# VectorE and ScalarE held to program order, softmaxes split in two, in a recurrent-memory attention kernel

## The chip, the cores and the metric

The kernel runs on one core of a Trainium2 chip. The metric is device microseconds of one execution; the figure before is the median of three runs. A separate execution was taken with the profiler, and everything read from a trace comes from that one.

## The reference

Two layers, twice: attention over segments of 32 tokens with 8 memory rows carried from segment to segment, then a gated feed-forward. All are residual, with a layer norm ahead. Sizes: 2048 tokens, width 448, 16 heads of 256, feed-forward width 1792.

```python
for s in range(n_seg):                       # 64 segments, one after another
    h = concat([mem, xs])                    # 8 memory rows + 32 tokens
    q, k, v = h @ Wq, h @ Wk, h @ Wv
    p = softmax(mask(q @ k.T) * scale)
    o = (p @ v) @ Wo
    mem = o[:8]                              # the next segment waits for this
    outs.append(o[8:])

x = x + A(layernorm(x)); x = x + B(layernorm(x))     # B: relu(x Wg) * (x Wu) @ Wd
x = x + A(layernorm(x)); x = x + B(layernorm(x))
```

## The kernel before

**Preparation.** For the first 80 us the kernel folds Wq with Wk and Wv with Wo into A_sb and B_sb (kept in SBUF). Then scores come from `h A h^T` and outputs from `(p h) B`; no separate q, k or v is formed.

**Steps.** The main loop runs 68 steps and a closing one. A step handles one segment of each of two chains: chain 0 is the first attention layer, chain 1 the second, four segments behind. Both share the weights, so one matmul has 80 columns: 2 x (8 + 32) rows. In the first and last four steps only one chain is active. Every second step has a feed-forward block of 128 rows (64 of each chain's), given by a `Feed` object `ff`: such a step is called a feed step here, the other a plain step.

**One step, in TensorE's order.** The heads go in two halves, `hf` 0 and 1.
- `project` (28 tiles a half, in five PSUM banks `BANKS`: tiles 0-5, 6-11, 24-27, 12-17, 18-23) makes `prj`, copied into TQ (tiles 0-23) and TZ (24-27). `project_early` does the narrow fourth chunk of four banks ahead of time in row pairs.
- `hk_make` turns the rows of h (tile kps) and copies them to `hk`.
- `late` is the end of the former step's `weigh_x(1)`, the y products.
- `scores_m` makes Sm, scores of the memory rows' queries; `scores_x` makes Sx, the cross scores of both chains' token rows. Each is followed by a softmax on VectorE and ScalarE: mx, se, exponential, ssum, rs and the weights, PM or PX.
- `flipped` turns the weights (tile pps) and copies them to PT. `weigh_m` multiplies them by hk (tiles ya, yb), `weigh_x` likewise (y1, y2, one for each chain); the results go to Y.
- `project_out` and `project_last` multiply Y by B_sb into ox and o3. From these come the next step's memory rows (in hT) and OT for the residual.

In a feed step the feed-forward comes between: `residual`, `norm` and `xposed` prepare xT; seven units of `gate_up` make ups, gps, the copy ut (ScalarE, two buffers) and hh (VectorE); `down` makes dps, `norm2` normalises for the second chain, `feed_on` puts the rows into hT.

**Order and buffers.** TensorE's order is the program's: `in_order` ties each matmul to the one before. VectorE's and ScalarE's instructions are placed by a scheduler of the language layer, which may take them out of program order; only the two halves of `normed` are pinned. PSUM has eight banks. `bank` gives a tile the bank that by a planned time is free first, where that time is the last matmul's plus `after` ns; a matmul on a bank waits for whoever read its former tile. A softmax was one call:

```python
def weights_of(Sp, n, dst, keep, tag, mask=None):   # mx, se, exp, ssum, rs, weights in one go
```

Of the kernel before, what the change touches and what calls it, by code (L numbers as in the profile page):

```python
# [15 lines left out]
DM = 448  # L16
# [4 lines left out]
SEG = 32  # L21
# [34 lines left out]
def build_kernel(ctx, tc, A_x, A_mem0, A_Wq, A_Wk, A_Wv, A_Wo, B_W_gate, B_W_up, B_W_down, out,  # L56
# [25 lines left out]

    now = [0]
# [38 lines left out]
    def evac(eng, dst, src):  # L122
        if eng is nc.scalar:
            nc.scalar.copy(dst, src)  # L124
        else:
            eng.tensor_copy(dst, src)  # L126
# [17 lines left out]
    nc.vector.tensor_scalar(out=rowi[:, 1:2], in0=rowi[:, 0:1], scalar1=3, scalar2=1,  # L144
                            op0=ALU.arith_shift_right, op1=ALU.bitwise_and)
    nc.vector.tensor_scalar(out=rowi[:, 2:3], in0=rowi[:, 0:1], scalar1=15, scalar2=None,
                            op0=ALU.bitwise_and)
    rowf = glob.tile([P, 3], F32, name="rowf")
    nc.vector.tensor_copy(rowf[:], rowi[:])
# [3 lines left out]
    nc.vector.tensor_copy(keyf[:, 0, :], keyi[:])  # L153
    nc.vector.tensor_scalar(out=keyf[:, 1, :], in0=keyf[:, 0, :], scalar1=-16.0, scalar2=None, op0=ALU.add)
    maskS = glob.tile([P, 4, L], BF, name="maskS")
    nc.vector.memset(maskS[:], 0.0)
    for b in range(4):
        o = 0 if b % 2 == 0 else MEM
        nc.vector.tensor_scalar(out=maskS[:, b, o:o + SEG], in0=keyf[:, b // 2, :], scalar1=rowf[:, 2:3],
                                scalar2=MASKVAL, op0=ALU.is_gt, op1=ALU.mult)  # L160

    blk = glob.tile([P, 2], F32, name="blk")
    nc.vector.tensor_copy(blk[:, 1:2], rowf[:, 1:2])
    nc.vector.tensor_scalar(out=blk[:, 0:1], in0=blk[:, 1:2], scalar1=-1.0, scalar2=1.0,
# [3 lines left out]
    nc.vector.memset(half[:], -0.5)  # L168
# [19 lines left out]
    def row_stats(t):  # L188

        stats = p_ln.tile([P, nc.vector.BN_STATS_DIM], F32, tag="ln_stats")  # L190
        nc.vector.bn_stats(stats[:], t[:])
        mv = p_ln.tile([P, 2], F32, tag="ln_mv")
        nc.vector.bn_aggr(mv[:], stats[:])  # L193
# [5 lines left out]
    def normed(stat):  # L199

        t, mv, rstd = stat
        xn = p_ln.tile([P, 512], BF, tag="ln_xn", bufs=3)
        for a, b, o in ((0, DM, 0), (384, DM, DM)):
            tc.keep_in_program_order(
                nc.vector.tensor_scalar(out=xn[:, o:o + b - a], in0=t[:, a:b], scalar1=mv[:, 0:1],
                                        scalar2=rstd[:], op0=ALU.subtract, op1=ALU.mult))
        return xn
# [21 lines left out]
    def set_mem(g, src, cs):  # L229

        nc.vector.tensor_copy(mem_of(g, cs)[:, 0:src.shape[1]], src)


    with tc.tile_pool(name="pre", bufs=6) as pre:
# [4 lines left out]
        for i in range(6):  # L239
            t = pre.tile([P, 4, 512], BF, name=f"nat{i}", bufs=1)  # L240
            (nc.gpsimd if i % 2 else nc.vector).memset(t[64:128, 3, :], 0.0)
            nats.append(t)
# [16 lines left out]
        spent = {nc.vector: 0.0, nc.scalar: 0.0}  # L259

        def share(dst, src, n, per):
            cost = {nc.vector: 60 + n * per[0], nc.scalar: 170 + n * per[1]}
# [27 lines left out]
        def first_rows():  # L290
# [4 lines left out]
            for b in range(2):  # L295
                rows_in(nc.vector, b, 0, tps0[:, :, block(b)])
# [3 lines left out]
            nc.vector.tensor_copy(mem0T[:], mtp[:])  # L300
# [107 lines left out]
    class Feed:  # L408
# [10 lines left out]
        def residual(self):  # L419
# [3 lines left out]
            nc.vector.tensor_tensor(self.x[:], tp[:].rearrange("p k d -> p (k d)")[:, 0:DM], self.x[:], op=ALU.add)  # L423
# [5 lines left out]
        def xposed(self):  # L429
            tps = transpose_tokens(self.xn)  # L430
            nc.vector.tensor_copy(xT[:], tps[:])

        def gate_up(self, u):
# [10 lines left out]
            nc.scalar.copy(ut[:, :, n], ups[:, :, n])  # L444
            nc.vector.scalar_tensor_tensor(out=hh[:, 2 * u:2 * u + 2, n], in0=gps[:, :, n], scalar=0.0,  # L445
                                           in1=ut[:, :, n], op0=ALU.max, op1=ALU.mult)

        def down(self):
# [4 lines left out]
            if self.first:  # L453
                nc.vector.tensor_tensor(self.nx[TB:P, :], dps[TB:P, 0:DM], self.x[TB:P, :], op=ALU.add)
                self.st = row_stats(self.nx)
                nc.sync.dma_start(xa[(i + 2) % 3][0:TB, :], self.nx[TB:P, :])
                if i + 3 < nblk:
                    nc.sync.dma_start(self.x[TB:P, :], x_dram[block(i + 3)])
            if self.second:
                nc.vector.tensor_tensor(self.x[0:TB, :], dps[0:TB, 0:DM], self.x[0:TB, :], op=ALU.add)  # L460
                nc.sync.dma_start(out_dram[block(i - LAG // BLK)], self.x[0:TB, :])

# [6 lines left out]
        def feed_on(self):  # L469
            if self.first:  # L470
                tps = transpose_tokens(self.xn)
                rows_in(nc.vector, self.i + 2, 1, tps[:, :, TB:P])
                rows_in(nc.scalar, self.i + 2, 0, tps[:, :, 0:TB])
# [22 lines left out]
    def project(hf, chains, hb, j, banks, pre={}):  # L496

        n = L * len(chains)
        for i0, k in banks:
# [8 lines left out]
            if i0 < 24:  # L508
                T = TQ[hf][:].rearrange("p g u w -> p g (u w)")[:, :, 16 * i0:16 * (i0 + k)]
                parts = [(nc.scalar if i0 % 12 else nc.vector, slice(0, P), T)]  # L510
            else:
                parts = [(nc.vector, slice(0, 64), TZ[hf][0:64, :, 0:64]),
                         (nc.scalar, slice(64, 128), TZ[hf][64:128, :, 64:128])]
# [15 lines left out]
    def weights_of(Sp, n, dst, keep, tag, mask=None):  # L529
# [3 lines left out]
        if mask is not None:  # L533
            nc.vector.tensor_tensor(se[:], Sp[:], mask, op=ALU.add)
            Sp = se
        nc.vector.tensor_reduce(mx[:], Sp[:], axis=AX.X, op=ALU.max)  # L536
        nc.vector.tensor_tensor(se[:], Sp[:], mx[:].unsqueeze(2).to_broadcast([P, n, L]), op=ALU.subtract)  # L537
        nc.scalar.activation(se[:], se[:], AF.Exp, scale=SCALE)  # L538
        ssum = main.tile([P, n], F32, tag=f"ssum{tag}", name="ssum")
        nc.vector.tensor_reduce(ssum[:], se[:], axis=AX.X, op=ALU.add)  # L540
        rs = main.tile([P, n], F32, tag=f"rs{tag}", name="rs")
        nc.vector.reciprocal(rs[:], ssum[:])
        if keep is not None:
            nc.vector.tensor_tensor(rs[:], rs[:], keep, op=ALU.mult)
        nc.vector.tensor_tensor(dst[:, :, 0:L], se[:], rs[:].unsqueeze(2).to_broadcast([P, n, L]), op=ALU.mult)

    def flipped(src, n, tag):
# [4 lines left out]
        nc.vector.tensor_copy(PT[:], pps[:].rearrange("p b q -> p (b q)"))  # L552
# [5 lines left out]
    def step(g, ff, pre, late):  # L558
# [12 lines left out]
        def ox_open():  # L571

            nonlocal ox
            ox = bank([P, 3, W], F32, "ox", hold=True) if not end else None

        def hk_make():
            kps = bank([P, 4, 128], BF, "kps")
            for i in range(4):
                tr(kps[:, i, :], hb[:, j, i * HI:(i + 1) * HI], ident[:])
            hk = HK[g % 2]  # L580
            nc.vector.tensor_copy(hk[:].rearrange("p k n -> p (k n)")[:, 0:DM],
                                  kps[:].rearrange("p k n -> p (k n)")[:, 0:DM])
            nc.scalar.copy(hk[:, 4, 64:128], kps[:, 3, 64:128])
            return hk

        def scores_m(hf):
            if not ms:
                return
# [3 lines left out]
            weights_of(Sp, 2, PM[hf], blk[:], f"m{hf}")  # L592

        def scores_x(hf):
            Sp = bank([P, 4, L], F32, "Sx", 900)
# [8 lines left out]
            return Sp  # L604

        def probs_x(hf, Sp):
            weights_of(Sp, 4, PX[hf], None, f"x{hf}", maskS[:] if len(chains) == 2 else None)

        def weigh_m(hf, hk, PT):
# [5 lines left out]
            nc.vector.tensor_copy(YB[hf][:, 0:16, M0:M0 + 16], ya[:].rearrange("p (t q) -> p t q", q=16))  # L615
# [4 lines left out]
            nc.scalar.copy(YB[hf][:, 16:28, M0:M0 + 16], yb[:].rearrange("p (t q) -> p t q", q=16))  # L620

        def weigh_x(hf, hk, PT):
# [14 lines left out]
            for c in chains:  # L637
                keep(nc.scalar if c == 0 else nc.vector, c, 0, y1[c][:])
# [24 lines left out]
        def project_last():  # L663
# [11 lines left out]
            nc.scalar.copy(os[0:64, lo:hi], o3[64:128, lo:hi])  # L675
            if ms:
                m0 = M0 + MEM * ms[0]
                nm = MEM * len(ms)
                nc.scalar.copy(os[64:128, m0:m0 + nm], o3[0:64, m0:m0 + nm])
                for e in range(2):  # L680
                    r = slice(64 * e, 64 * e + 64)
                    nc.vector.tensor_tensor(mem_of(g + 1, ms)[r, 3],
# [8 lines left out]
            for to, x in places:  # L691
                nc.vector.tensor_tensor(OT[r, 3, to:to + SEG], o3[r, x:x + SEG], os[r, x:x + SEG], op=ALU.add)

        def finish():
# [5 lines left out]
            if g == nsteps:  # L700
                nc.scalar.copy(OT[:, 0:3, 0:SEG], ox[:, :, XO[1]:XO[1] + SEG])
# [166 lines left out]
```

## Time and profile before

| what | value |
|---|---|
| median of 3 runs | 1687.98 us (1687.83 to 1688.02) |
| profiled execution | 1692.54 us, span 1690.2 us |
| TensorE matmul busy | 1624.2 us, 96% of the span |
| TensorE weight loads busy | 1484.2 us, 88% |
| VectorE busy | 1146.7 us, 68% |
| ScalarE busy | 661.6 us, 39% |
| granted TensorE clock | 0.993 |

In the groups of instructions, a line names where the operation stands in the code (for most matmuls the helper `mm`, L111, for turns `tr`, L119, for copies `evac`, L124 and L126), its output and inputs, shape and count, then busy time and mean length in ns, then the idle time of its engine just before and what ended it. In the timeline a row has start, length, engine, line and operation, and in brackets the idle time before it. Matmuls are pipelined: each shows as some 200 ns, while the next may start 36 ns later.

### The profile page before, as it was taken

The page shows a single profiled execution, that of the slowest core. Times are in us where ns is not written, and L with a number is a line of the kernel's source. Part 1 is how long each engine was busy: PE and PEld are TensorE (multiplying, and loading weights), DVE is VectorE, ACT ScalarE, POOL GpSimd, SP SyncE. Part 2 cuts the span into 40 slices and gives each one's busy share as a digit, 9 for nine tenths or more (in the row PEclk, how much of TensorE's full clock was granted, in tenths as well). Part 3 has the DMA queues.
Part 4 walks back from the last instruction along what each step waited for, and adds up shares of the span by engine and source line. Part 5 has one row for each costly group of instructions (what it writes and reads, how often), then busy time and mean ns, then how long its engine had stood idle before and what let it go on. Part 6 is the DMA issues. An engine that isn't in the chain of part 4 may idle for free.

```text
span 1690.2 us, 90175 instructions
## 1 busy us (share of the span) xinstructions
PE 1624.2 (96%) x41152; PEld 1484.2 (88%) x41152; DVE 1146.7 (68%) x4037; ACT 661.6 (39%) x1945; POOL 91.0 (5%) x178
## 2 busy tenths in 40 slices
PE   8999999999999999999999999999999999999997
PEld 6688899898988989989889899998889889898886
DVE  6765666776667667766676677666766667666774
ACT  5733433443334334433343334333343344333432
POOL 6200000000000000000000000000000000000000
PEclk9989999999999999999999999999999999999999
DMA  9330000000000000000000000000000000000000
GB/s 257 117 106 19 8 9 9 3 9 9 9 9 9 9 9 5 8 9 9 9 8 9 9 7 5 9 9 9 9 9 9 7 5 9 10 7 6 6 7 6
DMA packets 26782, 33.14 MB, mean 20 GB/s; under 512 B 3352, under 2 KB 24736, under 8 KB 26400
## 3 DMA queue, kind: packets, MB, share of 16 engines
q1 hardware_dynamic: 25312, 23.70, 5.1%
q8 instruction: 321, 5.26, 1.3%
q0 software_dynamic: 1088, 3.68, 0.7%
q14 instruction: 61, 0.50, 0.1%
HBM read 23.70 MB, written 1.84 MB: 15 GB/s over the span
## 4 chain that ended last, share of the span: by engine, by line
PE 80%; DVE 12%; ACT 5%; POOL 1%; issue 1%; ACTq 0%; POOLq 0%; DVEq 0%
PE prj L111 24%; PE ox L111 18%; PE ups L111 6%; PE gps L111 6%; PE dps L111 5%; PE o L111 4%; PE y L111 4%; ACT TQ L124 3%; PE Sx L111 2%; DVE ssum L540 2%; PE pps L119 2%; ACT se L538 2%; PE bps L111 1%; DVE TQ L126 1%; DVE mx L536 1%
## 5 line engine op out<-in xcount | busy, mean ns | idle before, releaser
L111 PE MATMUL prj<-hT,A_sb 128*128 128x80 bf16 (+3 forms) x15232 | 545.4, 199 | 0.1
L111 PEld LDWEIGHTS <-A_sb 128*128 128x128 bf16 (+1 forms) x15232 | 499.5, 99 | 22.8 <-issue 0.8
L111 PEld LDWEIGHTS <-B_sb 128*128 128x128 bf16 (+1 forms) x15232 | 491.1, 103 | 14.1 <-issue 0.4
L111 PE MATMUL ox<-Y,B_sb 128*128 128x80 bf16 (+4 forms) x11424 | 438.9, 199 | 0.3 <-issue 0.3
L126 DVE CAST Y<-y 128x128 bf16<-128x128 f32 (+2 forms) x384 | 156.6, 461 | 60.5 <-PE y L111 57.4
L124 ACT CAST TQ<-prj 128x480 bf16<-128x480 f32 (+2 forms) x304 | 147.6, 496 | 94.9 <-PE prj L111 93.1
L126 DVE CAST TQ<-prj 128x480 bf16<-128x480 f32 (+2 forms) x304 | 170.8, 567 | 14.2 <-PE prj L111 13.9
L124 ACT CAST Y<-y 128x512 bf16<-128x512 f32 (+2 forms) x384 | 144.1, 410 | 63.4 <-DVE Y L126 44.3
L111 PE MATMUL ups<-xT,Wu_sb 128*128 128x128 bf16 (+1 forms) x1904 | 141.0, 218 | 2.4 <-DVE se L537 1.9
L111 PE MATMUL gps<-xT,Wg_sb 128*128 128x128 bf16 (+1 forms) x1904 | 141.2, 218 | 0.0
L111 PEld LDWEIGHTS <-hk 40*128 40x128 bf16 (+1 forms) x1950 | 106.3, 96 | 34.9 <-issue 22.0
L538 ACT ACTIVATE se<-se 128x80 f32<-128x80 f32 (+1 forms) x270 | 80.2, 304 | 87.2 <-DVE se L537 85.3
L111 PEld LDWEIGHTS <-Wu_sb 128*128 128x128 bf16 x1904 | 111.2, 99 | 2.7 <-DVE se L537 2.0
L111 PEld LDWEIGHTS <-Wg_sb 128*128 128x128 bf16 x1904 | 112.9, 99 | 0.0
L675 ACT COPY os<-o 64x80 f32<-64x80 f32 (+3 forms) x68 | 14.8, 218 | 249.9 <-PE o L111 249.9
L444 ACT CAST ut<-ups 128x256 bf16<-128x256 f32 (+1 forms) x238 | 84.4, 355 | 70.1 <-PE ups L111 49.8
L445 DVE SCALAR_TENSOR_TENSOR hh<-gps,ut 128x256 bf16<-128x256 f32 (+1 forms) x238 | 93.1, 401 | 27.5 <-PE gps L111 16.7
L111 PE MATMUL y<-PT,hk 40*128 40x256 bf16 (+1 forms) x1280 | 100.3, 249 | 2.3 <-DVE PT L552 0.3
L195 POOL TENSOR_SCALAR rstd<-mv 128x1 f32<-128x1 f32 x67 | 14.8, 221 | 1533.7 <-DVE mv L193 1484.8
L111 PE MATMUL dps<-Wd_sb,hh 128*128 128x448 bf16 x476 | 95.7, 353 | 0.0
L124 ACT CAST TZ<-prj 64x320 bf16<-64x320 f32 (+2 forms) x152 | 55.9, 378 | 100.0 <-DVE TZ L126 39.0
L540 DVE TENSOR_REDUCE ssum<-se 128x2 f32<-128x80 f32 (+1 forms) x270 | 73.4, 274 | 31.2 <-ACT se L538 26.7
(120 smaller groups left out, 1964.7 us busy)
## 6 DMA issues: line engine op xcount, KB each, us to landing
wo<-in_A_Wo_dram POOLq DMA_DIRECT2D x8, 448.0 KB, 5.6
nat<-in_A_Wq_dram SPq DMA_DIRECT2D x8, 384.0 KB, 5.7
nat<-in_A_Wk_dram SPq DMA_DIRECT2D x8, 384.0 KB, 5.6
nat<-in_A_Wv_dram SPq DMA_DIRECT2D x8, 384.0 KB, 3.9
xa<-in_A_x_dram SPq DMA_DIRECT2D x32, 56.0 KB, 2.6
xa<-xp SPq DMA_DIRECT2D x32, 56.0 KB, 1.9
out_dram<-xa SPq DMA_DIRECT2D x32, 56.0 KB, 2.0
xp<-in_A_x_dram SPq DMA_DIRECT2D x30, 56.0 KB, 2.0
```

Source lines behind the costliest of these rows:

```text
L111: in_order(nc.tensor.matmul(out, lhsT, rhs, **k))
L119: in_order(nc.tensor.transpose(out, src, idn))
L124: nc.scalar.copy(dst, src)
L126: eng.tensor_copy(dst, src)
L195: nc.gpsimd.tensor_scalar(out=rstd[:], in0=mv[:, 1:2], scalar1=EPS, scalar2=None, op0=ALU.add)
L444: nc.scalar.copy(ut[:, :, n], ups[:, :, n])
L445: nc.vector.scalar_tensor_tensor(out=hh[:, 2 * u:2 * u + 2, n], in0=gps[:, :, n], scalar=0.0, in1=ut[:, :, n], op0=ALU.max, op1=ALU.mult)
L536: nc.vector.tensor_reduce(mx[:], Sp[:], axis=AX.X, op=ALU.max)
L538: nc.scalar.activation(se[:], se[:], AF.Exp, scale=SCALE)
L540: nc.vector.tensor_reduce(ssum[:], se[:], axis=AX.X, op=ALU.add)
L675: nc.scalar.copy(os[0:64, lo:hi], o3[64:128, lo:hi])
```

## The change

VectorE and ScalarE calls go through an `InOrder` wrapper that, from the first step of the main loop on, ties each instruction to the one before it on that engine. `weights_of` becomes `softmax`, which returns two functions: the first up to the exponential, the second from the sum to the weights. The step's order is rewritten:

- hk_make moves from behind bank 24 and bank 12 to right behind the first two banks, ahead of `residual`; in feed steps its large copy is ScalarE's.
- `norm` follows the five banks; `norm2` comes right after `down`.
- the memory scores of half 0 stand ahead of half 1's projections instead of behind the first bank; their second part follows two banks of these.
- in feed steps the second parts of the two other softmaxes stand among the first units, PM's turn after unit 3 instead of unit 4, and the second cross softmax after the last unit; in feed steps the copy of the tiles 12-17 of half 1 goes to ScalarE.
- in plain steps the turns and the second parts move as below.
- the two y2 copies of a chain go to one engine; the load of the next x block is written behind the store of the output; planned times of some banks are longer.

```diff
+    class InOrder:
+        def __init__(self, eng):
+            self.eng, self.last, self.on = eng, None, False
...
+            def call(*a, **k):
+                r = f(*a, **k)
+                if self.on:
+                    if self.last is not None:
+                        tc.add_manual_dep(r.ins, self.last,
...
+                    self.last = r.ins.name
+                return r
...
+    dve, act = InOrder(nc.vector), InOrder(nc.scalar)
...
         def down(self):
...
                 nc.sync.dma_start(xa[(i + 2) % 3][0:TB, :], self.nx[TB:P, :])
-                if i + 3 < nblk:
-                    nc.sync.dma_start(self.x[TB:P, :], x_dram[block(i + 3)])
             if self.second:
...
                 nc.sync.dma_start(out_dram[block(i - LAG // BLK)], self.x[0:TB, :])
+            if self.first and i + 3 < nblk:
+                nc.sync.dma_start(self.x[TB:P, :], x_dram[block(i + 3)])
...
-    def project(hf, chains, hb, j, banks, pre={}):
+    def project(hf, chains, hb, j, banks, pre={}, busy=False):
...
-                parts = [(nc.scalar if i0 % 12 else nc.vector, slice(0, P), T)]
+                parts = [(act if i0 % 12 or busy and hf and i0 else dve, slice(0, P), T)]
...
-    def weights_of(Sp, n, dst, keep, tag, mask=None):
+    def softmax(Sp, n, dst, keep, tag, mask=None):
...
+        def first():
+            src = Sp
+            if mask is not None:
+                dve.tensor_tensor(se[:], Sp[:], mask, op=ALU.add)
+                src = se
+            dve.tensor_reduce(mx[:], src[:], axis=AX.X, op=ALU.max)
+            dve.tensor_tensor(se[:], src[:], mx[:].unsqueeze(2).to_broadcast([P, n, L]), op=ALU.subtract)
+            act.activation(se[:], se[:], AF.Exp, scale=SCALE)
+
+        def second():
+            dve.tensor_reduce(ssum[:], se[:], axis=AX.X, op=ALU.add)
+            dve.reciprocal(rs[:], ssum[:])
+            if keep is not None:
+                dve.tensor_tensor(rs[:], rs[:], keep, op=ALU.mult)
+            dve.tensor_tensor(dst[:, :, 0:L], se[:], rs[:].unsqueeze(2).to_broadcast([P, n, L]), op=ALU.mult)
+
+        return first, second
...
-            ox = bank([P, 3, W], F32, "ox", hold=True) if not end else None
+            ox = bank([P, 3, W], F32, "ox", 1400, hold=True) if not end else None
...
-            nc.vector.tensor_copy(hk[:].rearrange("p k n -> p (k n)")[:, 0:DM],
-                                  kps[:].rearrange("p k n -> p (k n)")[:, 0:DM])
-            nc.scalar.copy(hk[:, 4, 64:128], kps[:, 3, 64:128])
+            evac(act if ff is not None else dve, hk[:].rearrange("p k n -> p (k n)")[:, 0:DM],
+                 kps[:].rearrange("p k n -> p (k n)")[:, 0:DM])
+            act.copy(hk[:, 4, 64:128], kps[:, 3, 64:128])
...
-            Sp = bank([P, 2, L], F32, "Sm", 900)
+            Sp = bank([P, 2, L], F32, "Sm", 1100)
...
-            Sp = bank([P, 4, L], F32, "Sx", 900)
+            Sp = bank([P, 4, L], F32, "Sx", 2500 if hf == 0 else 3500 if ff is None else 8000)
...
-                keep(nc.scalar if c == 0 else nc.vector, c, 16, y2[c][:, 0:256])
-                keep(nc.vector if c == 0 else nc.scalar, c, 24, y2[c][:, 256:384])
+                eng = dve if c or len(chains) == 1 else act
+                keep(eng, c, 16, y2[c][:, 0:256])
+                keep(eng, c, 24, y2[c][:, 256:384])
...
         project(0, chains, hb, j, BANKS[0:2], pre)
+        hk = hk_make()
         if ff is not None:
             ff.residual()
         next_piece()
-        project(0, chains, hb, j, BANKS[2:4], pre)
-        hk = hk_make()
+        project(0, chains, hb, j, BANKS[2:5], pre)
         if ff is not None:
             ff.norm()
-        project(0, chains, hb, j, BANKS[4:5], pre)
...
-        project(1, chains, hb, j, BANKS[0:1], pre1)
+        m0 = scores_m(0)
+        m0[0]()
+        project(1, chains, hb, j, BANKS[0:2], pre1)
+        m0[1]()
         next_piece()
-        scores_m(0)
-        project(1, chains, hb, j, BANKS[1:4], pre1)
+        project(1, chains, hb, j, BANKS[2:4], pre1, ff is not None)
...
-        Sx0 = scores_x(0)
+        x0 = scores_x(0)
         weigh_m(0, hk, pm)
-        scores_m(1)
-        Sx1 = scores_x(1)
-        probs_x(0, Sx0)
+        m1 = scores_m(1)
+        m1[0]()
+        x1 = scores_x(1)
+        x0[0]()
         if ff is not None:
-            feed(0, 1, 2, 3)
-            probs_x(1, Sx1)
+            feed(0)
+            m1[1]()
+            feed(1)
+            x0[1]()
+            feed(2, 3)
             next_piece()
+            pm = flipped(PM[1], 1, "m1") if ms else None
             feed(4)
-            pm = flipped(PM[1], 1, "m1") if ms else None
             px0 = flipped(PX[0], 2, "x0")
-            feed(5)
             weigh_m(1, hk, pm)
-            feed(6)
+            feed(5, 6)
+            x1[0]()
+            x1[1]()
             ox_open()
             project_out(0, 0, 8)
             next_piece()
             ff.down()
+            ff.norm2()
             project_out(0, 8, NT)
             project_last()
-            ff.norm2()
...
             ox_open()
-            project_out(0, 0, 20)
-            probs_x(1, Sx1)
-            project_out(0, 20, 23)
+            m1[1]()
+            x0[1]()
+            project_out(0, 0, 23)
             pm = flipped(PM[1], 1, "m1") if ms else None
+            project_out(0, 23, NT)
             px0 = flipped(PX[0], 2, "x0")
-            project_out(0, 23, NT)
             weigh_m(1, hk, pm)
+            x1[0]()
             next_piece()
+            x1[1]()
             project_last()
-            project_out(1, 0, 16)
+            project_out(1, 0, 22)
             px1 = flipped(PX[1], 2, "x1")
             next_piece()
-            project_out(1, 16, NT)
+            project_out(1, 22, NT)
...
+    dve.on = act.on = True
```

More of the change, by code (lines that the diff above doesn't have):

```diff
@@ L122, in evac @@
     def evac(eng, dst, src):
-        if eng is nc.scalar:
-            nc.scalar.copy(dst, src)
+        if eng is act:
+            act.copy(dst, src)
         else:
@@ L257, in load_nat @@
             return t
-        spent = {nc.vector: 0.0, nc.scalar: 0.0}
+        spent = {dve: 0.0, act: 0.0}
         def share(dst, src, n, per):
-            cost = {nc.vector: 60 + n * per[0], nc.scalar: 170 + n * per[1]}
+            cost = {dve: 60 + n * per[0], act: 170 + n * per[1]}
             eng = min(cost, key=lambda e: spent[e] + cost[e])
@@ L430, in xposed @@
             tps = transpose_tokens(self.xn)
-            nc.vector.tensor_copy(xT[:], tps[:])
+            dve.tensor_copy(xT[:], tps[:])
         def gate_up(self, u):
@@ L443, in gate_up @@
             ut = p_ut.tile([P, 2, 128], BF, tag="ut")
-            nc.scalar.copy(ut[:, :, n], ups[:, :, n])
-            nc.vector.scalar_tensor_tensor(out=hh[:, 2 * u:2 * u + 2, n], in0=gps[:, :, n], scalar=0.0,
+            act.copy(ut[:, :, n], ups[:, :, n])
+            dve.scalar_tensor_tensor(out=hh[:, 2 * u:2 * u + 2, n], in0=gps[:, :, n], scalar=0.0,
                                            in1=ut[:, :, n], op0=ALU.max, op1=ALU.mult)
@@ L551, in flipped @@
         PT = main.tile([P, n * 128], BF, tag=f"PT{tag}", name="PT")
-        nc.vector.tensor_copy(PT[:], pps[:].rearrange("p b q -> p (b q)"))
+        dve.tensor_copy(PT[:], pps[:].rearrange("p b q -> p (b q)"))
         return PT
@@ L674, in project_last @@
             os = main.tile([P, W], F32, tag="os", name="os")
-            nc.scalar.copy(os[0:64, lo:hi], o3[64:128, lo:hi])
+            act.copy(os[0:64, lo:hi], o3[64:128, lo:hi])
             if ms:
@@ L705, in finish @@
                 o2 = o + (TB if c == 0 else 0)
[L706 removed]
+                act.copy(OT[:, 0:3, o2:o2 + SEG], ox[:, :, XO[c]:XO[c] + SEG])
         def feed(*us):
```

93 lines of the change are left out of this document (42 added, 51 removed).

## The prediction

> **What bounds the kernel now.** I read the first part of the page, then the groups by form and the timeline of one pair of steps in the middle of the run.
>
> The page's first line on engines:
>
> ```profile
> PE 1624.2 (96%) x41152; PEld 1484.2 (88%) x41152; DVE 1146.7 (68%) x4037; ACT 661.6 (39%) x1945; POOL 91.0 (5%) x178
> ```
>
> TensorE bounds it: nothing is won but by taking pauses out of its queue. A matmul counts as busy for some 200 ns though the next starts 36 ns later, so short pauses hide in the 96%. They show in the weight loads (groups by form; the number after the last bar is idle time before the group):
>
> ```profile
> L119 PEld LDWEIGHTS <-PM 128*128 128x128 bf16 x134 | 13.1, 97 | 47.8 <-DVE PM L545 47.4 <-issue 0.3
> L119 PEld LDWEIGHTS <-xn 128*128 128x128 bf16 x268 | 17.2, 98 | 12.0 <-DVE xn L205 10.6
> L111 PEld LDWEIGHTS <-hk 128*128 128x128 bf16 x670 | 46.5, 97 | 11.0 <-issue 9.2 <-DVE PT L552 1.2
> ```
>
> The largest is the turning of PM, the memory weights: 47.8 us. The timeline of a plain step (start, length, instruction, idle before it) shows how it comes about:
>
> ```profile
> 928.97 0.23 DVE L540 TENSOR_REDUCE ssum<-se 128x2 f32<-128x80 f32 x1 [0.46 <-ACT se L538]
> 929.13 0.47 DVE L126 CAST TZ<-prj 64x320 bf16<-64x320 f32 x1
> ...
> 929.78 0.65 DVE L126 CAST TQ<-prj 128x480 bf16<-128x480 f32 x1
> ...
> 930.35 0.23 DVE L545 TENSOR_TENSOR PM<-se,rs 128x80 bf16<-128x80 f32 x1
> 930.64 0.10 PEld L119 LDWEIGHTS <-PM 128*128 128x128 bf16 x1 [0.73 <-DVE PM L545]
> ...
> 935.30 0.41 DVE L552 COPY PT<-pps 128x128 bf16<-128x128 bf16 x2
> 935.57 0.27 PE L111 MATMUL ya<-PT,hk 128*128 128x128 bf16 x2 [0.21 <-DVE PT L552]
> ```
>
> The softmax of the memory scores (mx at 928.01 to PM at 930.35) takes 2.6 us, since VectorE puts TZ and TQ copies between; TensorE has been through its projections since 929.87. Later ya waits for PT. In a feed step I look at the feed-forward stretch:
>
> ```profile
> 904.26 0.27 ACT L538 ACTIVATE se<-se 128x80 f32<-128x80 f32 x1 [0.59 <-DVE se L537]
> 904.44 0.35 ACT L444 CAST ut<-ups 128x256 bf16<-128x256 f32 x1
> ...
> 904.69 0.34 ACT L538 ACTIVATE se<-se 128x160 f32<-128x160 f32 x1
> ...
> 908.06 0.75 DVE L445 SCALAR_TENSOR_TENSOR hh<-gps,ut 128x256 bf16<-128x256 f32 x2
> ...
> 908.73 0.41 DVE L552 COPY PT<-pps 128x128 bf16<-128x128 bf16 x2
> ...
> 909.17 0.28 PE L111 MATMUL ya<-PT,hk 128*128 128x128 bf16 x2
> ```
>
> Here ya has no pause; the first ut copy goes between two exponentials; PT comes five units after the scores.
>
> **Rules of the sums.** From such rows: an independent instruction of VectorE or ScalarE starts about 0.08 us before the former's end (0.1 on ScalarE), a dependent one 0.04 after it, on either engine; a copy out of PSUM 0.25 to 0.29 after the last matmul's start; a matmul 0.05 after the copy it waits for. The run has 30 equal pairs of a plain (19.62 us) and a feed step (28.42); eight steps at the ends are shorter.
>
> **The memory scores ahead of the projections.** Before, 18 projections (0.65 us) stood between the y2 products and Sm, and 70 behind it; now Sm follows y2 and all 88 (3.17 us) come behind it. VectorE's list from there to PM in program order is two y copies (0.41, 0.28), mx 0.23, se 0.24, TQ 0.65, ssum 0.23, rs 0.15, product 0.16, PM 0.23. With overlaps and hops PM is done at 929.27 in the plain step; TensorE comes to it at 929.99. In the feed step it is 949.04 against 949.99. The pause goes: 0.76 us plain (last projection 929.84, turn 930.64, less 0.04), 0.69 feed. It stays gone while VectorE is less than 0.7 us late.
>
> **What that costs.** Sm takes the bank of y1_0 and so waits for ScalarE's copy of it; the 18 projections used to cover this. ScalarE has TQ (0.56) and then that copy (0.58): in the plain step TQ ends at 926.13, the copy at 926.63, Sm starts at 926.68, projections at 926.82; before, they started at 926.57 plus Sm's 0.14. That is +0.11. It includes the y2 pause (0.2 before, for the row copy; now for TQ). Were the copy on time it would be -0.1; were ScalarE one 0.38 copy further behind, +0.5. In the feed step mv stands ahead of the TZ copy and starts only when stats is through: TQ ends at 945.85, Sm is at 946.45, +0.21. The last TQ copy for the second memory scores ends about 0.07 late in feed steps: +0.07.
>
> **Row copies, projection copies and y copies elsewhere.** ScalarE has no 448-wide row copy before; a 256-wide COPY takes 372 ns and a 1024-wide one 1014, so 0.37 to 1.01, on a line between them 0.53. It sits under 52 projections and the next ScalarE copy waits for VectorE's TZ anyway, so even 1.01 costs nothing. One TQ copy per feed step goes from VectorE (645) to ScalarE (558): hidden, and in the 0.07. The y2 pieces change engines at 281 against 265 ns, which removes cross waits off the path: nothing.
>
> **Normalising earlier.** norm2 (0.39 + 0.29) now stands before the o3 additions, under 116 products of 3.3 us; the power on POOL ends before the o3 products do. xn no longer keeps tps waiting: 0.17 + 0.03 us, -0.20 per feed step. Behind it in VectorE's queue stand the memory additions, whose reader starts 3 us later: no cost. The x load is written behind the output store, but the listing of SP's queue has the same order: nothing.
>
> **Softmaxes in two parts, plain step.** PM1 is ready 0.4 us before its turn and PT before ya, since the second cross softmax no longer cuts in. The 0.42 between PT's request and ya falls to 0.04: -0.38. Y1's copy stands behind one more PT: +0.10 at o3.
>
> **Feed step.** Count from the start of the second cross scores. VectorE: Y copy to 0.40, mx and se to 0.82, the cross scores' add, mx, se to 1.74. ScalarE's exponential runs 1.77 to 2.11, and the first ut copy, in program order behind it, ends at 2.40; VectorE idles until then, its next instruction being hh. Then starts: hh 2.43, ssum 2.77, rs 3.04, product 3.22, PM 3.41, hh 3.56, ssum 3.90, rs 4.25, PX 4.45, hh 4.69, hh 5.03, PT 5.37 to 5.59. TensorE asks for PT after 0.41 of scores, ten half units of 0.444 and two turns (0.17): at 5.03, one unit sooner than before. ya waits +0.59. The second cross softmax comes behind the last hh (ends 8.3) and takes 2.4 us; the down product ends at 11.4, so it is covered by 0.7.
>
> That a waiting head holds a ready follower shows at 928.97: VectorE idles 0.46 us for ssum although the bank of the next TZ copy was full by 928.84 (its last projection starts near 928.56). The Trainium skill, "PSUM — Partial Sum Buffer", section "Engine vs sequencer instructions", says that VectorE's and ScalarE's queues are strict FIFO; the row agrees, and the rule speaks against this change. With it the feed term is +0.59; were the ut copy free to pass, the term would be about nothing and the whole sum 18 us lower.
>
> **Sum.** Plain: -0.76 + 0.11 - 0.38 + 0.10 = -0.93. Feed: -0.69 + 0.21 + 0.07 - 0.20 + 0.59 = -0.02. Thirty pairs: -28.5. The steps at the ends hold some 5 us of the PM idle; I take half: -2.5. Together -31. The profiled execution of 1692.5 (span 1690.2 and 2.3 around it) would become 1661.5; the median of the runs is 4.6 below the profiled one, so 1657.
>
> **Rivals.** First, PT is not late: ScalarE takes the exponential soon enough, or hops overlap more than I count. For: VectorE has 1.7 us less work in this stretch than before. Against: the order puts two hh ahead of PT. The gain is 31 + 30 x 0.59 = 49: 1639. 24%.
>
> Second, the gain is handed on: Sm waits longer for ScalarE, which has y copies of 0.58, 0.38 and 0.27 in line there, and each 0.1 us in both kinds of step is 6 us; and PT is late by 1 us instead of 0.59, 12 us. Sm 0.2 later and PT 1 us late give -31 + 12 + 12 = -7: 1681. For: ScalarE's waits are many and its order is now fixed. Against: its busy share is 39%. 16%, of which 4% lie within 0.2% and 2% above.
>
> Third, slower: ut and hh fall into lockstep in the feed step. There are two ut buffers, and the third ut must wait for the first hh; if each ut came only after the previous hh (ut 0.37, hh 0.42, two hops 0.08: 0.87 per unit), then hh number four would start at 2.43 + 3 x 0.87 and, with the two second softmax parts of about 0.8 each, at 6.6; PT ends at 7.2 and ya waits 2.2 instead of 0.59: +48, so 17 us slower than before, 1705. It decides from a PT 1.6 us late on. Against: the second ut is in ScalarE's queue right behind the first and needs no hh. 10%.
>
> That the order would not be what the diff says is out: the listing of the built queues shows it.
>
> **Numbers.** The forecast as summed has 50%; ya between 0.3 and 0.9 (9 us either way) and Sm's term 0.1 up or down (6 us) give 1642 to 1672 by themselves. The range reaches to the first rival's 1639 with 3 us for the ends, and to the second's 1681: 1636 to 1681. About 0.2% (3.4 us) is what a measurement can tell from no change. Faster 0.84 (0.50 + 0.24 + 0.10), the same 0.04, slower 0.12 (0.10 + 0.02).
>
> **What would show it.** Right: idle before the loads of PM under 6 us; a new wait of Sm on ScalarE's Y copy, about 0.2 us in each regular step; ya in feed steps waiting on PT, 15 to 20 us in all; plain steps near 18.7 us, feed steps near 28.4. Wrong: plain steps above 19.2, idle left at PM, pauses before ups or dps, or a ya without any wait in feed steps.

## The result, and the profile after

The changed kernel takes 1671.53 us (median of 4 runs, 1670.33 to 1672.79) against 1688.00 (1687.83 to 1689.07) for the kernel before on the same chip: a ratio of 0.9901, 95% interval 0.9884 to 0.9918. It is 16.5 us faster. The sign and the range held; the gain is about half of the 31 us forecast. The profiled execution took 1672.8, its span 1671.0 (before 1690.2) at a granted clock of 0.994 (before 0.993), a difference of 0.1%.

From the start of one plain step to the next, through one feed step, took 48.04 us before and takes 47.45 now, -0.59 where the prediction summed -0.95. Thirty times 0.59 is 17.7 of the 19.2 us by which the span fell. In what follows "the pair" is this time. Its two halves can't be compared singly: a step was measured from its first turn of h rows (tile kps), and the change puts that turn earlier in the step, in feed steps also past the residual's turn (0.23 us), which by this count moves from the plain step to the feed step. The prediction's "plain near 18.7, feed near 28.4" overlooked this. After the change they read 18.58 and 28.87.

The first part of the page of the changed kernel, engines with their busy time, share and instructions:

```profile
PE 1614.8 (97%) x41152; PEld 1485.6 (89%) x41152; DVE 1212.2 (73%) x3984; ACT 689.0 (41%) x1998; POOL 90.9 (5%) x178
```

TensorE's share hardly moves; as before, the pauses stand in the weight loads. The groups by form of the changed kernel (busy time, mean ns, then the idle time before the group and what ended it; L92 is the wrapper through which every VectorE and ScalarE call now goes, L134 the matmul helper, L142 the turns):

```profile
L142 PEld LDWEIGHTS <-PM 128*128 128x128 bf16 x134 | 13.3, 99 | 2.7 <-DVE PM L92 2.4
L142 PEld LDWEIGHTS <-xn 128*128 128x128 bf16 x268 | 17.2, 99 | 3.9 <-DVE xn L92 3.9
L134 PEld LDWEIGHTS <-hk 128*128 128x128 bf16 x670 | 47.0, 97 | 19.2 <-issue 18.7
L134 PE MATMUL ya<-PT,hk 128*128 128x128 bf16 x268 | 36.7, 218 | 14.3 <-DVE PT L92 14.2
L134 PE MATMUL Sm<-hT,TQ 128*128 128x80 bf16 x402 | 41.5, 200 | 17.4 <-ACT Y L92 13.3 <-ACT TQ L92 0.4
```

PM's idle time fell from 47.8 to 2.7 and xn's from 12.0 to 3.9. Two new waits stand against this: ya for PT in feed steps, and Sm for ScalarE's copy to Y. (The loads of hk hold the pause ahead of ya a second time; 19.2 and 14.3 are not to be added.)

The timeline of a plain step of the changed kernel (start, length, engine and operation, idle before it), where before TZ and TQ copies stood between the exponential and PM:

```profile
914.02 0.56 ACT L92 CAST TQ<-prj 128x480 bf16<-128x480 f32 x1 [0.35 <-PE prj L134]
914.35 0.65 PE L134 MATMUL y<-PT,hk 40*128 40x256 bf16 x10
914.77 1.03 ACT L92 CAST Y<-y 128x512 bf16<-128x512 f32 x3 [0.20 <-PE y L134]
...
915.41 0.27 PE L134 MATMUL Sm<-hT,TQ 128*128 128x80 bf16 x3 [0.40 <-ACT Y L92]
...
917.62 0.24 DVE L92 TENSOR_TENSOR PM<-se,rs 128x80 bf16<-128x80 f32 x1
917.78 0.48 DVE L92 CAST TZ<-prj 64x320 bf16<-64x320 f32 x1
...
918.66 0.10 PEld L142 LDWEIGHTS <-PM 128*128 128x128 bf16 x1
```

PM is done at 917.86 and TensorE comes to it at 918.66, 0.8 us of room. The price is in the upper half: ScalarE ends TQ at 914.58, stands idle for 0.20 until the y products are out, and only then copies; Sm waits for that copy, since it takes its bank.

The feed-forward stretch of a feed step:

```profile
940.60 0.34 ACT L92 ACTIVATE se<-se 128x160 f32<-128x160 f32 x1 [0.67 <-DVE se L92]
940.84 0.63 ACT L92 CAST ut<-ups 128x256 bf16<-128x256 f32 x2
941.23 0.42 DVE L92 SCALAR_TENSOR_TENSOR hh<-gps,ut 128x256 bf16<-128x256 f32 x1 [0.72 <-PE gps L134]
...
943.52 0.75 DVE L92 SCALAR_TENSOR_TENSOR hh<-gps,ut 128x256 bf16<-128x256 f32 x2
944.18 0.21 DVE L92 COPY PT<-pps 128x128 bf16<-128x128 bf16 x1
...
944.45 0.27 PE L134 MATMUL ya<-PT,hk 128*128 128x128 bf16 x2 [0.41 <-DVE PT L92]
```

The first ut copy stands behind the exponential, VectorE is idle for 0.72 us ahead of its first hh, and the delay runs on to PT and ya. The bracket puts those 0.72 down to the gate products, yet they end to the ut copy: a bracket names one of several semaphores. That it is the ut copy was argued from its end (about 941.2) and is tried below.

### The profile page after: what moved, and what is told of

Its sections match the earlier page's. It is cut to its first block, busy times and chain, and to the rows that moved or that the text cites. A ratio compares the mean times of both kernels' runs of the same rounds, so it can differ in the third digit from the quotient of the medians.

```text
span 1671.0 us, 90168 instructions
## 1 busy us (share of the span) xinstructions
PE 1614.8 (97%) x41152; PEld 1485.6 (89%) x41152; DVE 1212.2 (73%) x3984; ACT 689.0 (41%) x1998; POOL 90.9 (5%) x178
## 4 chain that ended last, share of the span: by engine, by line
PE 85%; DVE 7%; ACT 4%; POOL 2%; issue 1%; POOLq 0%; ACTq 0%; DVEq 0%
PE prj L134 24%; PE ox L134 24%; PE ups L134 6%; PE dps L134 5%; PE gps L134 5%; PE o L134 5%; PE Sx L134 3%; PE y L134 3%; ACT Y L92 2%; PE Sm L134 2%; PE ya L134 2%; PE bps L134 1%; DVE stats L92 1%; PE pps L142 1%; ACT TQ L92 1%
## 5 line engine op out<-in xcount | busy, mean ns | idle before, releaser
L134 PE MATMUL prj<-hT,A_sb 128*128 128x80 bf16 (+3 forms) x15232 | 530.2, 199 | 0.2 <-issue 0.2
L134 PEld LDWEIGHTS <-A_sb 128*128 128x128 bf16 (+1 forms) x15232 | 493.8, 99 | 16.2 <-issue 0.9
L134 PEld LDWEIGHTS <-B_sb 128*128 128x128 bf16 (+1 forms) x15232 | 491.1, 103 | 14.0 <-issue 0.4
L134 PE MATMUL ox<-Y,B_sb 128*128 128x80 bf16 (+4 forms) x11424 | 435.9, 199 | 0.4 <-issue 0.4
L92 DVE CAST Y<-y 128x256 bf16<-128x256 f32 (+2 forms) x400 | 160.9, 457 | 66.2 <-PE y L134 66.2
L92 ACT CAST TQ<-prj 128x480 bf16<-128x480 f32 (+1 forms) x340 | 162.2, 498 | 86.6 <-PE prj L134 84.6
L92 ACT ACTIVATE se<-se 128x80 f32<-128x80 f32 (+1 forms) x270 | 81.9, 303 | 212.2 <-DVE se L92 212.2
L92 DVE CAST TQ<-prj 128x480 bf16<-128x480 f32 (+2 forms) x268 | 150.1, 569 | 6.3 <-PE prj L134 5.7
L134 PEld LDWEIGHTS <-hk 40*128 40x128 bf16 (+1 forms) x1950 | 105.6, 96 | 44.7 <-issue 31.9
L134 PE MATMUL ups<-xT,Wu_sb 128*128 128x128 bf16 (+1 forms) x1904 | 140.8, 217 | 1.9 <-DVE hh L92 1.3
L134 PE MATMUL gps<-xT,Wg_sb 128*128 128x128 bf16 (+1 forms) x1904 | 140.9, 218 | 0.0
L92 ACT CAST Y<-y 128x256 bf16<-128x256 f32 (+1 forms) x368 | 129.6, 418 | 20.5 <-PE y L134 16.5
L92 DVE SCALAR_TENSOR_TENSOR hh<-gps,ut 128x256 bf16<-128x256 f32 (+1 forms) x238 | 93.8, 406 | 59.7 <-PE gps L134 53.2
L92 ACT CAST ut<-ups 128x256 bf16<-128x256 f32 (+1 forms) x238 | 81.8, 358 | 89.0 <-DVE hh L92 52.7
L134 PEld LDWEIGHTS <-Wu_sb 128*128 128x128 bf16 x1904 | 111.2, 99 | 2.4 <-issue 2.4
L134 PEld LDWEIGHTS <-Wg_sb 128*128 128x128 bf16 x1904 | 112.7, 99 | 0.0
L134 PEld LDWEIGHTS <-TQ 128*128 128x128 bf16 x1938 | 86.8, 97 | 27.4 <-issue 11.8
L92 DVE COPY PT<-pps 128x128 bf16<-128x128 bf16 (+1 forms) x270 | 68.7, 254 | 49.5 <-PE pps L142 48.1
L134 PE MATMUL y<-PT,hk 40*128 40x256 bf16 (+1 forms) x1280 | 99.3, 248 | 4.0 <-ACT Y L92 0.6
L92 ACT CAST TZ<-prj 64x320 bf16<-64x320 f32 (+2 forms) x152 | 55.9, 378 | 98.7 <-DVE TZ L92 96.5
L134 PE MATMUL dps<-Wd_sb,hh 128*128 128x448 bf16 x476 | 96.2, 354 | 0.0
```

The lines of the kernel that those rows point to most:

```text
L92: r = f(*a, **k)
L134: in_order(nc.tensor.matmul(out, lhsT, rhs, **k))
```

## The experiments

Each kernel ran beside the kernel before on its chip (1689.8 to 1690.6 there), so ratios to it are compared; the changed kernel's is 0.9901. "The pair" counts as above: 48.04 before, 47.45 after.

**The late PT, asked later.** The first two look at the wait of ya in feed steps. This one takes the pause away from TensorE's side, with one more unit ahead of ya.

```diff
-            weigh_m(1, hk, pm)
-            feed(5, 6)
+            feed(5)
+            weigh_m(1, hk, pm)
+            feed(6)
```

> The changed kernel with one statement moved: in feed steps weigh_m(1), whose ya waits for PT behind two hh, comes one feed-forward unit (0.89 us of TensorE) later. My theory: the changed kernel's feed step loses 0.55 us a step (30 steps) at ya because PT stands behind two hh on VectorE; then ya has no wait here, 16 us are won and the time is about 1655 us (changed kernel 1671.5). Rival: VectorE is the bound of this stretch, and TensorE waits for hh or Y a little later instead: 1666 to 1672.

1652.05 us, ratio 0.9775 (0.9760 to 0.9789); the pair 46.87, 0.58 less. The group of ya lost its idle time:

```profile
L134 PE MATMUL ya<-PT,hk 128*128 128x128 bf16 x268 | 36.6, 218 | 1.6 <-DVE PT L92 1.4
```

The whole wait was worth 0.58 a feed step and nothing took its place.

**The late PT, its cause.** The same wait from the other side: only the exponential of the first cross softmax is issued behind the first ut copy.

```diff
...
             feed(0)
+            x0[2]()        # the exponential, no longer in x0[0]
             m1[1]()
...
```

> The changed kernel with the exponential of the cross softmax of half 0 issued behind the first ut copy in feed steps; nothing else. My theory: the 0.7 us in which VectorE idles for the first hh comes from ScalarE's order (ut behind an exponential that waits for VectorE); then the first hh starts about 0.7 us sooner, PT with it, the pause at ya shrinks from 0.55 to below 0.1 us and the time is 1655 to 1658 us. Rival: PT is late because of the two hh and of the two ut buffers, whatever the exponential does: the first hh comes sooner, ya waits 0.3 us or more, 1663 to 1672.

1652.34 us, 0.9775 (0.9759 to 0.9792); the pair 46.87. The timeline of this kernel at the same place:

```profile
928.56 0.37 ACT L92 CAST ut<-ups 128x256 bf16<-128x256 f32 x1
929.09 0.42 DVE L92 SCALAR_TENSOR_TENSOR hh<-gps,ut 128x256 bf16<-128x256 f32 x1
929.27 0.34 ACT L92 ACTIVATE se<-se 128x160 f32<-128x160 f32 x1 [0.34 <-DVE se L92]
...
932.10 0.21 DVE L92 COPY PT<-pps 128x128 bf16<-128x128 bf16 x1
...
932.55 0.27 PE L134 MATMUL ya<-PT,hk 128*128 128x128 bf16 x2
```

ut goes first, the exponential fills ScalarE's gap, and ya follows PT without a pause. One instruction of 0.34 us, standing in wait for VectorE ahead of a copy that was ready, cost 0.58 a feed step. Cause and price of this term are shown.

**The statements without the order.** The changed program with VectorE and ScalarE left to the scheduler (the two halves of `normed` pinned as before).

```diff
-    dve.on = act.on = True
```

> The changed kernel's statements with the program order of VectorE and ScalarE not enforced, so that the scheduler places them as in the kernel before. My theory: the statements alone win the PM pause only in feed steps (in plain steps the TQ copy of tiles 12-17 is placed ahead of PM again: about 0.4 us, 12 us in all), PT of the plain step comes behind the second cross softmax again (0.38 us, 11 us), while ya in feed steps no longer waits (-16 us): 1678 us, between 1673 and 1684. Rival A: enforced order is what pays, so it is back near 1688. Rival B: the order of statements decides alone: 1671.

1697.31 us, 1.0042 (1.0028 to 1.0057); the pair 48.40. Rival A comes nearest, and the kernel is even slower than before. The scheduler again puts copies of TZ and TQ between the sum and PM, as the timeline of a plain step of this kernel shows:

```profile
929.49 0.23 DVE L92 TENSOR_REDUCE ssum<-se 128x2 f32<-128x80 f32 x1 [0.60 <-ACT se L92]
929.64 0.47 DVE L92 CAST TZ<-prj 64x320 bf16<-64x320 f32 x1
...
930.30 0.65 DVE L92 CAST TQ<-prj 128x480 bf16<-128x480 f32 x1
930.87 0.23 DVE L92 TENSOR_TENSOR PM<-se,rs 128x80 bf16<-128x80 f32 x1
...
931.15 0.10 PEld L142 LDWEIGHTS <-PM 128*128 128x128 bf16 x1 [0.73 <-DVE PM L92]
```

PM's idle time in this kernel's groups is 33.2 us. About a third of the gain at PM is left, while Sm still waits for the Y copy:

```profile
PE Sm L134 <- ACT Y L92: 22.7, 60, 0.4
```

**The order without the statements.** The program of before, with the wrapper and the planned times of the Sx banks from the change, nothing moved.

```diff
...
+    dve, act = InOrder(nc.vector), InOrder(nc.scalar)
...
+    dve.on = act.on = True
...
```

> The kernel before, its statements as they were, with VectorE and ScalarE held to program order (and the planned times of the Sx banks as in the changed kernel, since the banks would lock otherwise). My theory: order without the split softmaxes is dear. PM of half 0 comes in time, but VectorE then waits at each exponential and PT for ya stands behind all the softmaxes: some 3 us at ya in plain steps, 1.5 us of hh in feed steps: 1750 to 1830 us. Rival: order alone brings the gain, the rest of the change little: 1665 to 1690.

1914.55 us, 1.133 (1.1314 to 1.1347), worse than expected. PM's idle time is down to 5.9 here too, but each softmax is issued in one go and VectorE now waits for every exponential: 105.9 us in 270 waits, against 26.7 in 61 before. What stands behind waits along. TensorE's waits in this kernel (total, times, longest):

```profile
PE ya L134 <- DVE PT L92: 133.9, 134, 1.7
PE ups L134 <- DVE hh L92: 51.8, 33, 2.9
PE pps L142 <- DVE PX L92: 43.7, 35, 1.9
```

And VectorE's for the exponentials, in the kernel before and in this one:

```profile
DVE ssum L540 <- ACT se L538: 26.7, 61, 0.5
DVE ssum L92 <- ACT se L92: 105.9, 270, 0.5
```

So neither half of the change pays alone: statements +0.4%, order +13%, both -1.0%. In the whole change the same waits for exponentials come to 29.4 us.

**The memory scores' place.** Sm and its first part go back behind the first bank of half 1, the second part behind the second bank. This gives Sm's wait its old cover and takes 0.65 us from the softmax's time.

```diff
+        project(1, chains, hb, j, BANKS[0:1], pre1)
         m0 = scores_m(0)
         m0[0]()
-        project(1, chains, hb, j, BANKS[0:2], pre1)
+        project(1, chains, hb, j, BANKS[1:2], pre1)
```

> The changed kernel with the memory scores of half 0 back behind the first bank of half 1 (their place before), still in two parts. My theory: Sm then no longer waits for the y copy (0.33 us a step, 20 us in all), but PM and behind it, in program order, the TZ and TQ copies come later: the pause at PM is below 0.1 us, ya of half 0 in plain steps waits 0.6 us instead of 0.06, the second memory scores in feed steps wait 0.6 instead of 0.16. The two sides nearly cancel: 1671 to 1690 (changed kernel 1671.5). Rival: the early place is the mistake, and without it the time falls by the whole 20 us to about 1652.

1694.41 us, 1.0027 (1.0017 to 1.0037); the pair 48.18. The waits of Sm for the Y copy are gone, and others stand in their place:

```profile
PE ya L134 <- DVE PT L92: 28.4, 69, 0.6
PE Sm L134 <- ACT TQ L92: 13.9, 60, 0.3
```

The early place is worth 21 us more than its wait costs. The time lies just above the 1671 to 1690 expected, and the rival is out. PM itself waits only 4.0 us here; the loss is handed on to ya and to the second Sm.

**Between the two places.** With the later ya kept, Sm goes behind the first 9 of half 1's projections (0.32 us).

```diff
...
-        project(1, chains, hb, j, BANKS[0:2], pre1)
+        project(1, chains, hb, j, BANKS[0:1], pre1, among=memory_scores)   # called after 3 tiles
+        project(1, chains, hb, j, BANKS[1:2], pre1)
...
```

> The kernel with ya one unit later (1652.05 us) in which nine of the first bank's 18 projections (0.33 us) stand ahead of the memory scores of half 0, where TensorE now waits for ScalarE's y copy. My theory: the wait is 0.45 us in plain and 0.25 to 0.35 us in feed steps and these projections run inside it; PM has 0.8 us to spare, so 0.3 us a step and about 16 us are won: 1634 to 1640. Rival: Sm waits for something that moves along with it (TQ, the y products), and the time stays within 4 us of 1652.

1645.95 us, 0.9736 (0.9722 to 0.9751); steps 18.36 and 28.29, the later ya alone 18.58 and 28.29. The plain step gains 0.22, the feed step nothing: less than the theory's 0.3 a step, and with 6 us in all also more than the 4 that the rival allows. In the plain step TensorE still comes to Sm 0.18 us after the projection before it, where projections follow each other in 0.04. The timeline of a feed step shows where that went:

```profile
921.07 0.42 ACT L92 CAST TZ<-prj 64x320 bf16<-64x320 f32 x1 [0.93 <-DVE TZ L92]
921.52 1.02 ACT L92 CAST TQ<-prj 128x480 bf16<-128x480 f32 x2
...
922.59 0.21 PE L134 MATMUL Sm<-hT,TQ 128*128 128x80 bf16 x1 [0.19 <-ACT TQ L92]
```

The second memory scores come sooner, but ScalarE's two TQ copies for them do not: they stand behind TZ, and TZ waits 0.93 us for VectorE's half of the same bank, which stands behind m0's second part.

**TZ ahead of the second part.** So m0's second part goes behind the bank of tiles 24-27, in every step, on top of the former.

```diff
-        m0[1]()
         next_piece()
-        project(1, chains, hb, j, BANKS[2:4], pre1, ff is not None)
+        project(1, chains, hb, j, BANKS[2:3], pre1, ff is not None)
+        m0[1]()
+        project(1, chains, hb, j, BANKS[3:4], pre1, ff is not None)
```

> The kernel with nine projections ahead of Sm, in which the second part of the first memory softmax also comes behind the bank of tiles 24-27, so that VectorE's TZ copy precedes it. My theory: the wait of the second memory scores in feed steps (0.16 us) hangs on ScalarE's TZ copy, which waits for VectorE's; TZ comes some 0.4 us sooner, the wait goes and 4 to 6 us are won against the same kernel without this. Rival: PM now comes late (its margin is 0.4 us) and a pause at its turn returns: 0 to 10 us slower.

1647.22 us, 0.9746 (0.9731 to 0.9760); steps 18.69 and 28.04. Both theories held, one in each kind of step: the feed step gains 0.25, the plain step loses 0.33, because PM is late again:

```profile
L142 PEld LDWEIGHTS <-PM 128*128 128x128 bf16 x134 | 13.0, 97 | 11.9 <-DVE PM L92 11.1 <-issue 0.3
```

**The same in feed steps only.** The edit is shown against the kernel just above.

```diff
+        if ff is None:
+            m0[1]()
         next_piece()
...
-        m0[1]()
+        if ff is not None:
+            m0[1]()
```

> Nine projections ahead of Sm, ya one unit later, and the second part of the first memory softmax behind the bank of tiles 24-27 in feed steps alone. My theory: the plain step keeps 18.36 us (PM has no time to spare for TZ there), the feed step takes 28.04 instead of 28.29, since in it the second memory scores wait for the TZ and TQ copies in line: 30 x 0.25 = 7.5 us less than nine projections alone, 0.9691 of the kernel before, some 1638 us. Rival: the two gains are the same wait and do not add: 0.973 or above.

1639.01 us (1637.18 to 1639.37), 0.9697 (0.9681 to 0.9714); steps 18.36 and 28.04. This is the fastest version run, 3.0% below the kernel before. The groups of its three former waits:

```profile
L134 PE MATMUL Sm<-hT,TQ 128*128 128x80 bf16 x402 | 38.3, 201 | 0.2
L134 PE MATMUL ya<-PT,hk 128*128 128x128 bf16 x268 | 36.6, 218 | 1.4 <-DVE PT L92 1.2
L142 PEld LDWEIGHTS <-PM 128*128 128x128 bf16 x134 | 13.1, 98 | 3.3 <-DVE PM L92 2.6
```

**The small terms.** Three kernels undo one edit of the change each. First, norm2 goes back behind `project_last`:

```diff
-            ff.norm2()
             project_out(0, 8, NT)
             project_last()
+            ff.norm2()
```

> The changed kernel with norm2 back behind the o3 products. My theory: the pause of tps for xn (0.2 us in each of 30 feed steps) comes back, 6 us slower than the changed kernel: 1675 to 1680. Rival: with VectorE in program order xn is early enough either way: within 2 us of 1671.5.

1678.85 us, 0.9931 (0.9916 to 0.9946); the pair 47.66, 0.21 more, for a predicted 0.20. The wait is back where it was before (12.0):

```profile
L142 PEld LDWEIGHTS <-xn 128*128 128x128 bf16 x268 | 17.2, 98 | 12.5 <-DVE xn L92 11.2
```

Second, the large hk copy of feed steps on VectorE, as before:

```diff
-            evac(act if ff is not None else dve, hk[:]...
+            evac(dve, hk[:]...
```

> The changed kernel with the large row copy of feed steps on VectorE instead of ScalarE. My theory: it stands ahead of the residual addition there and puts the TZ copy back by about 0.1 us, and with it TQ, the y copy and Sm: 2 to 4 us slower than the changed kernel. Rival: the row copy's engine does not matter, as the prediction had it: within 2 us. Second rival: ScalarE's load is what delays Sm, and the move wins 5 us or more.

1673.26 us, 0.9898 (0.9883 to 0.9913): by its time not to be told from the change. Its trace has the feed step 0.07 longer, 2 us in all. That is the lower end of what was expected from the undoing, but one trace does not settle so small a term.

Third, the TQ copy of tiles 12-17 on VectorE in feed steps:

```diff
-        project(1, chains, hb, j, BANKS[2:4], pre1, ff is not None)
+        project(1, chains, hb, j, BANKS[2:4], pre1)
```

> The changed kernel with the copy of tiles 12-17 of half 1 on VectorE in feed steps, as it is in plain steps. My theory: VectorE has time for it before PT can start, ScalarE's last TQ copy comes sooner and the 0.16 us wait of the second memory scores goes: 2 to 5 us faster than the changed kernel. Rival: VectorE is late for PT of half 0 then, and ya waits: 5 us slower or more.

1667.70 us, 0.9866 (0.9852 to 0.9881); the feed step is 0.09 shorter, 2.7 us of the some 6. So the change's move of that copy to ScalarE costs time. The other 3 us lie outside the regular steps or in the spread of the runs; which of the two stays open. It was not run together with the fastest version.

## Why the prediction was right, and where it was not

| term, us per step | predicted | measured | read from |
|---|---|---|---|
| PM's pause, plain / feed | -0.76 / -0.69 | -0.76 / -0.60 | last projection to turn: 0.80 / 0.63 before, 0.04 / 0.04 now |
| Sm behind the Y copy, plain / feed | +0.11 / +0.21 | +0.34 / +0.34 | both timelines |
| second memory scores, feed | +0.07 | +0.15 | pause from 938.58 to 938.76 |
| ya, plain | -0.38 | -0.36 | 0.42 after the turn before, 0.06 now |
| ya, feed | +0.59 | +0.57; 0.58 when removed | timeline; two experiments |
| o3, plain | +0.10 | +0.05 | 56 products in 1.05 instead of 1.00 |
| tps, feed | -0.20 | -0.20; 0.21 when undone | xn group; experiment |
| small changes of spacing, not forecast | 0 | about -0.1 | the rest |
| sum of the pair | -0.95 | -0.59 | step lengths |

**The step that failed** is the term of Sm: "in the plain step TQ ends at 926.13, the copy at 926.63, Sm starts at 926.68", and its twin for the feed step. In the plain step it timed the copy by when ScalarE is free, and not by when the bank is full. In the trace of before, ScalarE was done with the row copy at 926.19 and began the copy of the y products only at 926.27, 0.30 after the last product of that bank had started (925.97). In the plain step of the changed kernel ScalarE stands idle for 0.20 between TQ and that copy. In the feed step it is ScalarE that is late:

```profile
932.69 0.42 ACT L92 CAST TZ<-prj 64x320 bf16<-64x320 f32 x1 [1.01 <-DVE TZ L92]
933.13 0.56 ACT L92 CAST TQ<-prj 128x480 bf16<-128x480 f32 x1
933.63 1.07 ACT L92 CAST Y<-y 128x512 bf16<-128x512 f32 x3
...
934.27 0.27 PE L134 MATMUL Sm<-hT,TQ 128*128 128x80 bf16 x3 [0.15 <-ACT Y L92]
```

TZ waits 1.01 us for VectorE's half of the bank, and TQ and Y stand behind it. TQ ends 0.53 us after the first y product starts (933.16); the prediction's 945.85 lies 0.38 after that of the kernel before (945.47). One thing that it did not count shows in the trace: the row turns now stand ahead of the residual's turn, which so comes 0.23 later against the y products (2.62 us before them instead of 2.85), and with it the chain of stats, mv and VectorE's TZ copy. No run tries this alone.

From the last projections of half 0 to the first full-rate ones of half 1, Sm included, it took 1.43 and 1.49 us before and takes 1.77 and 1.82 now: some 0.34 more in each. That is 0.36 us a pair more than forecast (0.23 and 0.13), or 10.8 us of the 14.5 by which the median exceeds 1657. The misses of the other terms go both ways and cancel, which is luck. The wait itself is shown by the kernel that puts Sm between the two places: its plain step has 0.22 of the 0.34 less. Of the feed step the same edit won nothing before TZ went ahead, so there the price is shown only by the two edits together (0.25).

**A size read from one step.** PM's pause in feed steps was put at 0.69. That is what the feed step around 902 shows (0.73 from the last projection to the turn, less 0.04), and this step is the odd one. In 28 of the 30 regular feed steps of the kernel before, the turn comes 0.63 after the last projection, so the pause was worth 0.60, and 2.7 us less in all. The loads of PM in the two steps:

```profile
902.33 0.10 PEld L119 LDWEIGHTS <-PM 128*128 128x128 bf16 x1 [0.67 <-DVE PM L545]
950.37 0.10 PEld L119 LDWEIGHTS <-PM 128*128 128x128 bf16 x1 [0.56 <-DVE PM L545]
```

**The ends and the offset.** The steps at the ends were taken at -2.5 and gave about -1.5. The prediction also carried the 4.6 us by which the profiled execution of before lay above the median of its runs; the changed kernel's profiled execution lies 1.3 above. That is 3.3 us which belong to no mechanism.

**What held.** The feed term came out by the list of starts that the prediction wrote down: hh behind the ut copy, and ya late by 0.57. Its reading of the Trainium skill, "PSUM — Partial Sum Buffer", section "Engine vs sequencer instructions" (VectorE's and ScalarE's queues are strict FIFO), is borne out here: the ut copy, whose products were ready, stayed behind the waiting exponential, and with the two exchanged in the listing the 0.58 were gone. The first rival (PT not late, 1639) fell with the 14.3 us at ya. The second (the gain handed on) was right in kind for Sm, by 0.23 and 0.13 instead of 0.2 each, and wrong for PT, which stayed at 0.57 instead of 1. The third (ut and hh in lockstep) did not come about: the second ut follows the first at once, x2 in one row of 0.63. Later ut copies do wait for hh (52.7 us in 88 waits), but for the hh two units back, and so each is done before its own hh begins (the third ends at 942.11, its hh starts at 943.52).

The zero-cost claims: the row copy on ScalarE was worth at most 2 us. The move of the TQ copy was counted as "hidden, and in the 0.07"; it was not hidden, and of the 0.15 measured there 0.09 goes with it. The second cross softmax behind the last hh caused no pause ahead of dps.

## What to carry to other kernels

Program order on two engines is worth only what the order of the statements is worth: the same wrapper made one listing 13% slower and the other 1.4% faster than that listing without it (0.9901 against 1.0042). In a strict order, an instruction that waits for another engine must not stand ahead of a ready one that somebody needs; look for such pairs where two engines hand work to and fro. When a wait is taken away, work out the next one from both of its conditions, the engine free and the operand there, because the later one decides; the best version came from following a wait three times from place to place until nearly all of it lay under other work. And read the size of a pause in more than one step before it goes into a sum.

## What the runs showed of the hardware that was not expected

VectorE's busy time rose from 1146.7 to 1212.2 us with less work in it: the lengths of its instructions add up to 1353.5 us before and 1340.4 after. The busy time counts overlapping instructions once. With the scheduler left free, the changed statements show 1131.4 (lengths 1327.5); the old statements in program order show 1237.2 (1364.5). So the order makes the difference: with it, VectorE's instructions overlap less (that this is because more of them follow the one they depend on is argued, not shown). An engine's busy share is then no measure of its work, and the rise from 68% to 73% went along with a faster kernel.
